# Seven products for a second expert, chosen ahead; the overflow counts among the experts' work

## The chip, the cores and the metric

The kernel runs on one core of a Trainium2 chip. The metric is the time of one execution in microseconds, as the device reports it. Five engines work in parallel, each through its own instructions in program order: TensorE (PE, with its weight loads as PEld), VectorE (DVE), ScalarE (ACT), GpSimd (POOL) and SyncE (SP). They wait for each other and for DMA transfers by semaphores.

## The reference

Sliding-window attention over 8 batches of 8 heads, 576 positions of 64 values, is followed by a mixture of 8 experts in which every token goes to one expert only.

```python
scores = scale * np.matmul(q, k.transpose(0, 1, 3, 2))      # 8 x 8 x 576 x 576
mask = (rel >= 0) & (rel < window)                           # window 128
scores = np.where(mask, scores + bias[None], -1000000000.0)
...
return np.matmul(attn, v).astype(np.float32)
...
expert_idx = np.argmax(logits, axis=1)                       # 4608 tokens of 512, 8 experts
gate_w = probs[np.arange(N), expert_idx]
for e in range(E):
    mask = expert_idx == e
    h = np.maximum(x[mask] @ w1[e], 0.0)                     # w1: 512 x 1024
    out[mask] = gate_w[mask, None] * (h @ w2[e])             # w2: 1024 x 512
```

Nothing fixes beforehand which expert gets how many tokens.

## The kernel before

**Attention.** 36 tiles of 128 tokens pass one after the other through scores, softmax, weights times values, and routing. The rows of a tile go, as two fp16 halves (`hi` and `lo`, whose sum is the fp32 value), into a table `xs` in DRAM that is sorted by expert; GpSimd scatters them (`put`, L940). After 24 tiles the most frequent expert so far is chosen (`head_ops`, eight small VectorE operations, L404 to L411). Its weights are fetched in 16 pieces (`stg`, L985) and split into `hi` and `lo` by ScalarE (L988) and VectorE (L992). Its first 384 rows are computed while attention still runs, to fill TensorE (`head_hidden`, L1020; `head_output`, L1044; `y_head`, L1050). When all tiles are routed, `rank_ops` sorts the experts by their counts.

**Experts.** Each expert has a fixed number of row slots (`SLOTS`, 672 for expert 0, 688 for expert 1) and its turn (`TURNS = [0, 1, 4, 3, 5, 6, 2, 7]`; 0 is the one begun in attention, 1 the next largest by count). SyncE writes a guard of zeros behind the expert's rows (L1350), reads the rows back transposed (`xT`, L1364 and L1367), reads token numbers and gates (`info`), and fetches weights (`ws`, by expert numbers that it loads from memory). Then comes the hidden layer and then the output layer (`ps2` at L1733, 24 matmuls of 512 columns for each block of 128 rows), then `y` and a scattering `put` (L452).

**Two forms of the hidden layer.** `hidden` (L1556) is plain: for each of 8 blocks of 128 hidden units, 12 matmuls over each column block (4 pieces of the sum, each as `hi`·`hi`, `hi`·`lo`, `lo`·`hi`). `seven` (L1576) cuts rows and weights into halves and makes seven products where eight stand in the plain form: for each of 4 pairs of blocks (`ft`), 7 products of 6 matmuls, each over half of the expert's rows. That needs sums of weight quarters (`t1` to `t4`), sums of row halves (`z`, split into `S`), and for every `ft` five combinations of the products on VectorE (`combine`: `u2`, `u3`, `c22`, `c21`, `c12`, L1587 and L1588). `PLAIN = 2` gives the first two experts in turn the plain form. Within an `ft` the products come in the order a(x), b(S2), d(S3), c(S1), a(x), d(x), c(S4); the sixth adds into the bank d, which `u3` must have read before.

**What sets the order.** A planner (`Plan`) takes jobs with an engine, a cost in nanoseconds, what they follow, and a due time, and writes out one static order for every engine; `fill=True` jobs go where the planner sees the engine free. One plan orders attention, a second one the experts.

**The end.** Behind the plan of the experts stand 22 VectorE operations that count the blocks of 128 rows by which an expert overflows its slots (`ovr` to `ooi`, L2041 to L2085), and a loop over these blocks, which these inputs never enter. The last expert also has its output layer in seven products (L1658, with combinations at L1666 and L1667). After the first `put` of the last expert GpSimd drains its queue (`drain`, L1753).

## Time and profile before

| | |
|---|---|
| median of 3 runs | 616.57 us (614.1 to 617.86) |
| profiled execution | 614.46 us |
| its span, first to last instruction | 612.8 us |
| TensorE busy | 581.9 us, 95% |
| VectorE busy | 507.4 us, 83% |
| ScalarE, GpSimd busy | 391.5 us, 315.2 us |
| mean granted TensorE clock | 0.998 of full speed |

The span is what the profile shows; the execution's own time is 1.66 us more. Attention fills the span up to about 262 us, the first expert's remaining rows run to 295, the second expert's from 295 to 349, and the other six to the end. Busy time is an engine's time in instructions. Instructions on one engine overlap a little, so that the start of one to the start of the next can be less than the length of the first.

### The profile page before, as it was taken

The numbers are of one execution on the slowest core, as the hardware profiler recorded it, in microseconds if no ns is written. First come the engines' busy times: TensorE is split into PE (matmuls) and PEld (weight loads), VectorE is DVE, ScalarE is ACT, GpSimd is POOL, SyncE is SP. The second block draws the span as 40 slices with busy tenths as digits, with TensorE's granted clock in tenths as the row PEclk, the third lists the DMA queues.
The fourth block names the chain that finished last, engine by engine and source line by source line (L and its number), as shares of the span: only waits on it lengthen the run. The fifth ranks groups of instructions, "written<-read, shape, count | busy, mean of one in ns | idle before, by whom it ended". The sixth has DMA issues, their size and how long they took to land.

```text
span 612.8 us, 17588 instructions
## 1 busy us (share of the span) xinstructions
PE 581.9 (95%) x6661; PEld 403.3 (66%) x6661; DVE 507.4 (83%) x1259; ACT 391.5 (64%) x895; POOL 315.2 (51%) x486
## 2 busy tenths in 40 slices
PE   7999989999898888999999999999999999999995
PEld 4787777777776666545664584574674854754885
DVE  4988898899999899826489589789899898789692
ACT  6999898899897895415256149149266383376541
POOL 7878779978887888730212402401606214108442
PEclk9999999999999999999999999999999999999999
DMA  9999989999999997779977908908929669424101
GB/s 187 203 174 189 209 184 232 194 203 214 213 187 236 263 173 92 269 196 240 245 211 209 322 15 249 290 1 231 293 55 334 150 150 314 95 76 115 66 2 70
DMA packets 224760, 112.65 MB, mean 184 GB/s; under 512 B 196758, under 2 KB 200342, under 8 KB 224673
## 3 DMA queue, kind: packets, MB, share of 16 engines
q1 hardware_dynamic: 214512, 85.24, 64.5%
q0 software_dynamic: 10160, 26.26, 15.3%
q8 instruction: 53, 0.87, 0.6%
q14 instruction: 35, 0.28, 0.2%
HBM read 72.93 MB, written 19.70 MB: 151 GB/s over the span
## 4 chain that ended last, share of the span: by engine, by line
PE 52%; DVE 24%; ACT 7%; DMA 6%; POOL 5%; issue 4%; POOLq 0%; ACTq 0%; DVEq 0%
PE ps L1733 20%; PE ps7d L1576 5%; PE ps7c L1576 5%; PE ps7a L1576 5%; PE ps L1556 5%; DVE pq L552 4%; DVE nm L693 3%; DVE sc L686 3%; DMA xT<-gx 3%; PE ps7b L1576 3%; ACT pe L700 2%; ACT pq L549 2%; PE ps_t L1723 2%; DMA stg<-moe_w_dram 2%; DVE xf L798 2%
## 5 line engine op out<-in xcount | busy, mean ns | idle before, releaser
L452 POOL DMA_INDIRECT out_dram<-y,ids x32 | 62.1, 1941 | 204.2 <-ACT y L1745 137.0
L700 ACT ACTIVATE pe<-sc,nm 128x128 f32<-128x128 f32 x288 | 84.8, 386 | 6.8 <-DVE nm L693 4.0
L1733 PE MATMUL ps<-w2h,hl 128*128 128x512 f16 x224 | 84.9, 379 | 0.5 <-DVE hl L1697 0.5
L1733 PE MATMUL ps<-w2h,hh 128*128 128x512 f16 x224 | 84.9, 379 | 0.0
L1733 PE MATMUL ps<-w2l,hh 128*128 128x512 f16 x224 | 84.9, 379 | 0.0
L1733 PEld LDWEIGHTS <-hh 128*128 128x128 f16 x448 | 43.7, 98 | 51.7 <-issue 0.8
L1576 PEld LDWEIGHTS <-w1h 128*128 128x128 f16 x672 | 65.7, 98 | 14.8 <-issue 0.3
L552 DVE SCALAR_TENSOR_TENSOR pq<-ptp,pq 128x512 f16<-128x512 f32 x72 | 53.0, 736 | 13.1 <-ACT pq L549 13.0
L549 ACT ACTIVATE pq<-ptp 128x512 f16<-128x512 f32 x72 | 55.4, 769 | 10.9 <-PE ptp L708 7.8
L708 PE MATMUL ptp<-ident,pe 128*128 128x128 f32 x288 | 47.9, 284 | 12.8 <-DVE pq L552 5.1
L676 PE MATMUL sc<-kh,qh 64*64 64x192 f32 (+3 forms) x1280 | 58.1, 289 | 0.0
L693 DVE TENSOR_REDUCE nm<-sc 128x2 f32<-128x256 f32 x144 | 55.8, 411 | 0.6 <-PE sc L676 0.6
L676 PEld LDWEIGHTS sc<-kh,qh 64*64 64x64 f32 (+1 forms) x1280 | 45.0, 139 | 8.8 <-issue 3.6
L825 POOL TENSOR_TENSOR gx<-xf,gx 128x512 f16<-128x512 f32 x36 | 42.3, 1175 | 8.4 <-DVE gx L814 7.4
L708 PEld LDWEIGHTS ptp<-ident,pe 128*128 128x128 f32 x288 | 31.6, 140 | 21.4 <-ACT pe L700 12.4
L1745 ACT ACTIVATE y<-ps,gs 128x512 f32<-128x512 f32 x24 | 16.3, 681 | 45.1 <-PE ps L1733 39.3
L776 PE MATMUL av<-vh,mp 128*128 128x65 f16 (+1 forms) x512 | 42.9, 196 | 1.2 <-POOL mp L728 0.8
L625 POOL TENSOR_TENSOR vo<-ldv,vh 128x512 f16<-128x512 f32 x36 | 40.8, 1137 | 6.3 <-ACT vh L617 5.8
L940 POOL DMA_INDIRECT xs<-gx,di x36 | 36.8, 1021 | 10.6 <-issue 6.0
L1556 PE MATMUL ps<-xT,w1h 128*128 128x288 f16 (+2 forms) x192 | 39.8, 302 | 1.4 <-DMA xT<-xs 1.4
L686 DVE COPY_PREDICATED sc<-mask_full,sc 128x256 f32<-128x256 int32 x96 | 38.2, 418 | 3.1 <-PE sc L676 3.1
L1733 PEld LDWEIGHTS <-hl 128*128 128x128 f16 x224 | 21.9, 98 | 27.7 <-DVE hl L1697 1.5
(315 smaller groups left out, 1743.0 us busy)
## 6 DMA issues: line engine op xcount, KB each, us to landing
ws<-moe_w_dram SPq DMA_DIRECT2D x46, 512.0 KB
ldk<-k_dram SPq DMA_DIRECT2D x32, 256.0 KB
ldq<-q_dram SPq DMA_DIRECT2D x32, 256.0 KB
ldv<-v_dram SPq DMA_DIRECT2D x32, 256.0 KB
...
```

Of the source, the lines that this page charges most:

```text
L452: ins = nc.gpsimd.indirect_dma_start(out[:, :], bass.IndirectOffsetOnAxis(ap=ids, axis=0), y, None, bounds_check=NTOK - 1, oob_is_err=False)
L549: nc.scalar.activation(hi, ps, AF.Copy, scale=scale)
L552: nc.vector.scalar_tensor_tensor(lo, ps, scale, hi, op0=ALU.mult, op1=ALU.subtract)
L676: nc.tensor.matmul(sc[T, hf, j][o, l, c], qT[T]["h"][rows, hp, o], x["h"][rows, hp, c.start + at : c.stop + at], start=False, stop=True, s ...
L686: nc.vector.copy_predicated(ps[:, :, 0:P], m, ps[:, :, P : 2 * P])
L693: nc.vector.tensor_reduce(nm_t[T, hf, j], sc[T, hf, j][:, :, 0:P], axis=AX.X, op=ALU.min)
L700: nc.scalar.activation(pr_t[T, hf][:, 2 * l + j, :], ps[:, l, 0:P], AF.Exp, bias=nm[:, l : l + 1], scale=-1.0)
L708: nc.tensor.transpose(pt[:, i, :], pe[:, i, :], ident)
L776: nc.tensor.matmul(o_, a_, b_, start=False, stop=(n == last), skip_group_check=True)
L1556: nc.tensor.matmul(ps[:, :w], a[:, kt, fs], xx[:, b + kt, c0 : c0 + w], start=(n == 0), stop=(n == len(jobs) - 1))
L1576: nc.tensor.matmul(ps, a[:, idx, c, fs], b[:, c, :], start=(n in OPENS and m == 0), stop=(m == len(jobs) - 1), skip_group_check=True)
L1733: nc.tensor.matmul(ps, x[:, ft, a * P : (a + 1) * P], w[:, ft, c], start=(n == 0), stop=(n == len(jobs) - 1))
```

## The change

Expert 1, the second in turn, gets seven products (`PLAIN = 1`). Nine small VectorE operations (`second_ops`) choose it in attention from the same counts after 24 tiles, and `rank_ops` then keeps it in second place. Its four weight quarters 11, 12, 21 and 22 are fetched at the head of SyncE's stream for the experts, and all four sums of quarters are formed on VectorE (for the other experts `t1` and `t3` are summed by accumulating DMAs). The rows of an expert with seven products are read in two jobs, odd half first, and each half is summed (`rebuild`) as it comes. The overflow counts become filler jobs of the experts' plan, allowed from the second expert's first rows of `hl` on. `y_head` and its `put` go from attention's plan to the experts' plan. The pools stand in another order, so that the weights of the first expert with seven products lie where tiles of attention lay. Attention and experts stand in one region of manual order.

```diff
-PLAIN = 2
+PLAIN = 1
...
+    def second_ops():
+        V = nc.vector
+
+        def k1(nm, dt=F32):
+            return kt_(nm, [P, 1], dt)
+
+        def ke(nm):
+            return kt_(nm, [P, E])
+
+        return [
+            lambda: V.scalar_tensor_tensor(ke("sc"), ke("ho"), -float(PAD), ke("hc"), op0=ALU.mult, op1=ALU.add),
+            lambda: V.tensor_reduce(k1("sm"), ke("sc"), axis=AX.X, op=ALU.max),
+            lambda: V.scalar_tensor_tensor(ke("sd"), ke("sc"), k1("sm"), desc_e, op0=ALU.is_ge, op1=ALU.mult),
+            lambda: V.tensor_reduce(k1("sw"), ke("sd"), axis=AX.X, op=ALU.max),
+            lambda: V.tensor_scalar(ke("so"), ke("sd"), k1("sw"), None, op0=ALU.is_equal),
+            lambda: V.tensor_tensor(ke("si"), ke("so"), iota_e, op=ALU.mult),
+            lambda: V.tensor_reduce(k1("sf"), ke("si"), axis=AX.X, op=ALU.add),
+            lambda: V.tensor_copy(k1("se", I32), k1("sf")),
+            lambda: V.scalar_tensor_tensor(ke("hs"), ke("ho"), 2.0, ke("so"), op0=ALU.mult, op1=ALU.add),
+        ]
...
-            ("DVE", 90, lambda: V.scalar_tensor_tensor(ke("key"), ke("ho"), float(PAD), ke("key"), op0=ALU.mult, op1=ALU.add)),
+            ("DVE", 90, lambda: V.scalar_tensor_tensor(ke("key"), ke("hs"), float(PAD), ke("key"), op0=ALU.mult, op1=ALU.add)),
...
+                prev = [f"head{len(ops) - 2}"]
+                for i, f in enumerate(second_ops()):
+                    J(f"second{i}", "DVE", 90, f, after=prev, due=due("route", u) + 30000 + 150 * i, fill=True)
+                    prev = [f"second{i}"]
             if tail:
-                prev = [done]
+                prev = [done, f"second{len(second_ops()) - 1}"]
...
-            J(f"y{a}", "ACT", 600, lambda a=a: head_y(a), after=[f"out{a}_5", "head_info"] + [f"fetch{i}" for i in range(NP)], makes=[("stg", ("y", a))], uses=[("ps2", a)], due=2e7)
-            J(f"yput{a}", "POOL", 1200, lambda a=a: head_put(a), after=[f"y{a}", (f"put{NT - 1}", ORDER)], uses=[("y", a)], due=3e7)
...
+        steps = [
+            (90, lambda: V.tensor_tensor(ovr, nk, capt, op=ALU.subtract)),
+            (100, lambda: V.tensor_scalar(it128, it, float(P), None, op0=ALU.mult)),
+            (
+                450,
+                lambda: V.tensor_tensor(
+                    big, ovr.unsqueeze(2).to_broadcast([P, E, MAXOV]), it128.unsqueeze(1).to_broadcast([P, E, MAXOV]), op=ALU.is_gt
+                ),
+            ),
+            (450, lambda: V.tensor_reduce(nb, big, axis=AX.X, op=ALU.add)),
...
+            *pick(oe, eb),
+            *pick(oo, base),
+            *pick(on, nk),
...
-        xt, yp, st, ht, wT, wS, zp = (
+        xt, yp, st, wS, zp, wT, ht = (
             pool(*a)
-            for a in (("xt", 2), ("yp", 3), ("wstage", WSTG), ("ht", 1), ("wthird", 1), ("wseven", 1), ("xsum", 1))
+            for a in (("xt", 2), ("yp", 3), ("wstage", WSTG), ("wseven", 1), ("xsum", 1), ("wthird", 1), ("ht", 1))
...
+                number = sel_["se"][0:1, 0:1] if s == TURNS[1] else ebi[0:1, s : s + 1]
+                state[s] = dict(e=nc.sync.value_load(number, min_val=0, max_val=E - 1))
...
-                dl = [nc.sync.dma_start(xx[:, :, t, :], halves[t].bitcast(F16), transpose=True) for t in range(2)]
+                if odd:
+                    xx = xx[:, :, 0 : 2 * n2].rearrange("p k (t j) -> p k t j", t=2)
+                    d = nc.sync.dma_start(xx[:, :, 1, :], halves[1].bitcast(F16), transpose=True)
+                    for p_ in scatters:
+                        sync_dep(d, p_)
+                    state[s]["xT"] = xx
+                    return
+                xx = state[s]["xT"]
+                dl = [nc.sync.dma_start(xx[:, :, 0, :], halves[0].bitcast(F16), transpose=True)]
...
+            if s == TURNS[1]:
+                a, b = {"t1": ("12", "11"), "t3": ("12", "22"), "t2": ("t3", "11"), "t4": ("t2", "21")}[what]
+                nc.vector.tensor_tensor(stage(s, what)[0], ws[s, a], ws[s, b], op=ALU.add)
...
-        def rebuild(s, d):
+        def rebuild(s, t):
             h, xx = SLOTS[s] // 2, state[s]["xT"]
             if s not in zs:
                 zs[s] = zp.tile([P, 2, 2, 2, MH], F32, tag="z", name=f"z_{s}")
-            x, y = (xx[:, b + 2 * d : b + 2 * d + 2, :, 0:h] for b in (0, KT))
-            (nc.gpsimd if XSUM == "POOL" else nc.vector).tensor_tensor(zs[s][:, d, :, :, 0:h], x, y, op=ALU.add)
+            x, y = (xx[:, b : b + KT, t, 0:h] for b in (0, KT))
+            z = zs[s].rearrange("p d k t j -> p (d k) t j")[:, :, t, 0:h]
+            (nc.gpsimd if XSUM == "POOL" else nc.vector).tensor_tensor(z, x, y, op=ALU.add)
...
+            J(f"yh{a}", "ACT", 600, lambda a=a: head_y(a), early=handed["out"][a], makes=[("y", ("yh", a))], uses=[("pre", 8 - HEAD // P + a)], due=-1e6)
+            J(f"yhput{a}", "POOL", 1200, lambda a=a: head_put(a), after=[f"yh{a}"], uses=[("yh", a)], due=-1e6, dma=750)
...
-                first_gets = [("q", what) for what in ("t3", "t1", "11", "21", "22")] if seven_ else [(1, c) for c in range(4)]
+                first_gets = [("q", what) for what in (("t3", "t1", "11", "21", "22") if p > 1 else ("11", "12", "21", "22"))] if seven_ else [(1, c) for c in range(4)]
                 later_gets = [("q", "o" + what) for _, what in first_gets] if s == DEEP else [(2, c) for c in range(4)]
                 for n, (w_, c) in enumerate(first_gets + later_gets):
-                    d = (lead - 3000 * (not seven_) if n < len(first_gets) else m) + 1500 * n
+                    d = (lead if p > 1 else -1e6) + 1500 * n if n < len(first_gets) else (m if p > 1 else 0) + 1500 * n
...
+        caps, steps = over_ops()
+        J("over", "POOL", 600, caps, due=1e6)
+        for i, (ns, f) in enumerate(steps):
+            J(
+                f"over{i}", "DVE", ns, f, after=[f"over{i - 1}" if i else "over", f"qlo{TURNS[PLAIN]}_0a"], port=True, fill=True,
+                due=1e6 + i,
+            )
         plan.run(handed["free"])
...
-    ovr = ot.tile([P, E], F32, name="ovr")
-    nc.vector.tensor_tensor(ovr, nk, capt, op=ALU.subtract)
...
+    with tc.manual_schedule():
+        with ExitStack() as actx:
+            attention(actx)
+        ebi, nki, eb, nk = (sel_[n] for n in ("ebi", "nki", "eb", "nk"))
+        with ExitStack() as mctx:
+            moe(mctx)
```

On SyncE, at the seam between attention and experts, before; `stg` is the last weight piece of expert 0, `xT` the transposed rows of expert 0:

```order
L985 ISA
L985 DMA stg_6898<-moe_w_dram 128x512
L1349 TENSOR_LOAD nki
L1349 ISA x2
L1350 ISA
L1350 DMA xs<-zrow 32x514
L1367 ISA
L1367 DMA_TRANSPOSE xT_7190<-xs 128x8x288
L1383 ISA
L1383 DMA info_7191<-xs 128x2x2
```

and with the change, at the same place:

```order
L1006 ISA
L1006 DMA stg_6916<-moe_w_dram 128x512
L1425 TENSOR_LOAD se
L1425 ISA x2
L1540 ISA
L1540 DMA ws_1_7186<-moe_w_dram 128x2x512
L1540 ISA
L1540 DMA ws_1_7188<-moe_w_dram 128x2x512
L1540 ISA
L1540 DMA ws_1_7190<-moe_w_dram 128x2x512
L1540 ISA
L1540 DMA ws_1_7192<-moe_w_dram 128x2x512
```

The load of the second expert's number and the four quarters now stand ahead of the load of the counts (`nki`), of the guard and of expert 0's transposed rows, which follow behind these rows.

On VectorE, at the end of expert 0's hidden layer, before; `hl` is the low half of its hidden values, `w2l` the low half of expert 1's second weights:

```order
L1697 SCALAR_TENSOR_TENSOR hl_7242<-ps_0_384_7_7380,hh_7241 128x288
L1707 COPY th_7414<-hh_7241 128x256
L1707 COPY tl_7415<-hl_7242 128x256
L1531 SCALAR_TENSOR_TENSOR w2l_7409<-ws_1_0_7276,w2h_7408 128x1024
L1531 SCALAR_TENSOR_TENSOR w2l_7409<-ws_1_1_7282,w2h_7408 128x1024
L1531 SCALAR_TENSOR_TENSOR w2l_7409<-ws_1_2_7406,w2h_7408 128x1024
L1747 TENSOR_SCALAR y_3_7498<-ps_0_3_0_7418,gs_7211 128x512
```

and with the change, from the sum of expert 1's second row half on:

```order
L1590 TENSOR_TENSOR z_7395<-xT_7304 128x4x344
L1626 SCALAR_TENSOR_TENSOR w2l_7492<-ws_1_0_7413,w2h_7491 128x1024
L1596 TENSOR_TENSOR z_7395<-z_7395 128x2x344
L1626 SCALAR_TENSOR_TENSOR w2l_7492<-ws_1_1_7417,w2h_7491 128x1024
L1842 TENSOR_SCALAR y_3_7517<-ps_0_3_0_7466,gs_7263 128x512
L1596 TENSOR_TENSOR z_7395<-z_7395 128x2x344
L1604 TENSOR_TENSOR S_7435<-z_7395,S_7435 128x688
L1596 TENSOR_TENSOR z_7395<-z_7395 128x2x344
L1604 TENSOR_TENSOR S_7435<-z_7395,S_7435 128x688
L1626 SCALAR_TENSOR_TENSOR w2l_7492<-ws_1_2_7433,w2h_7491 128x1024
L1604 TENSOR_TENSOR S_7435<-z_7395,S_7435 128x688
L1626 SCALAR_TENSOR_TENSOR w2l_7492<-ws_1_3_7438,w2h_7491 128x1024
```

Ahead of the same `w2l` splits there is now the summing and splitting of expert 1's rows, in turn with them. Then come eight small operations on `info`, of which the last two are shown with the first combinations of expert 1:

```order
L1510 SCALAR_TENSOR_TENSOR ids_0_7264<-got_5_7605,far_5_7604 64x1
L1511 TENSOR_SCALAR gs_0_7265<-info_7361 64x1
L1682 TENSOR_TENSOR u_1_0_7630<-ps7b_0_7577,s_1_0_7587 128x344
L1682 TENSOR_TENSOR u_1_0_7632<-ps7d_0_7589,u_1_0_7630 128x344
L1683 SCALAR_TENSOR_TENSOR ps7b_0_7577<-ps7c_0_7612,u_1_0_7632 128x344
```

`u` in the third and fourth row are `u2` and `u3`; they stand behind all four `w2l` and all eight `info` operations.

On VectorE, near the end of the last expert, before; `u` and `r` are the combinations `u2` and `u3` of the output layer, the rows of L2072 and L2073 are overflow counts:

```order
L2073 TENSOR_REDUCE oe<-in_11244 128x44
L1666 TENSOR_TENSOR u_7_('o', 0)_11063<-ps2b_0_11041,r_10728 128x256
L2072 TENSOR_TENSOR in_11244<-inn,base 128x352
L2083 CAST oei<-oe 128x44
L2073 TENSOR_REDUCE oo<-in_11244 128x44
L1666 TENSOR_TENSOR r_10728<-ps2d_0_11054,u_7_('o', 0)_11063 128x256
L2072 TENSOR_TENSOR in_11244<-inn,nk 128x352
L1667 SCALAR_TENSOR_TENSOR ps2b_0_11041<-ps2c_0_11027,r_10728 128x256
L1666 TENSOR_TENSOR ps2e_0_10990<-ps2e_0_10990,r_10728 128x256
```

and with the change:

```order
L1727 SCALAR_TENSOR_TENSOR hs_3_11069<-ps7c_3_11014,hs_3_11069 128x256
L1761 TENSOR_TENSOR u_7_('o', 0)_11151<-ps2b_0_11129,r_10816 128x256
L1761 TENSOR_TENSOR r_10816<-ps2d_0_11142,u_7_('o', 0)_11151 128x256
L1762 SCALAR_TENSOR_TENSOR ps2b_0_11129<-ps2c_0_11115,r_10816 128x256
L1761 TENSOR_TENSOR ps2e_0_11078<-ps2e_0_11078,r_10816 128x256
L1762 SCALAR_TENSOR_TENSOR ps2c_0_11115<-ps2c_0_11115,u_7_('o', 0)_11151 128x256
```

The counts are gone from between the combinations.

## Rows read from the trace of the kernel before

**Rows 1.** The page, busy time of each engine, its share of the span, and instructions.
```profile
PE 581.9 (95%) x6661; PEld 403.3 (66%) x6661; DVE 507.4 (83%) x1259; ACT 391.5 (64%) x895; POOL 315.2 (51%) x486
```

**Rows 2.** Busy time by stretch: length; PE, PEld, DVE, ACT, POOL; clock, DMA share, GB/s.
```profile
200.00:240.00 40.00, 33.69 (x662) 26.08 (x662) 37.50 (x117) 34.32 (x94) 33.62 (x54) 1.00 0.96 183
...
260.00:270.00 10.00, 10.00 (x48) 4.47 (x46) 2.06 (x13) 1.37 (x2) 4.39 (x8) 1.00 0.55 151
...
400.00:460.00 60.00, 60.00 (x413) 40.23 (x411) 55.34 (x108) 34.85 (x62) 13.11 (x8) 1.00 0.55 150
```

**Rows 3.** The chain of work, 288 to 352 us: start, length, what.
```profile
294.93 28.00 PE ps L1556 x192
322.93 25.90 PE ps L1733 x120
348.83 0.69 PE ps7a L1576 x6
```

**Rows 4.** What TensorE waited for, 225 to 613 us: total, times, longest.
```profile
PE ps L1556 <- DMA xT<-xs: 1.4, 1, 1.4
...
PE ps2c L1658 <- DVE ps2b L1667: 0.9, 1, 0.9
...
PE ps L1733 <- DVE hl L1697: 0.5, 1, 0.5
```

**Rows 5.** The chain of work, 235 to 300 us.
```profile
249.46 5.61 DMA stg<-moe_w_dram
...
271.41 7.28 DMA out_dram<-y_head,ids_head
278.87 1.06 ACT w1h L1533
...
285.27 1.47 PE ps L1733 x6
286.77 8.16 PE ps L1733 x37
```

**Rows 6.** SyncE's queue in order of time, 248 to 300 us: start, time to issue, what.
```profile
263.41 0.38 SPq L1350 DMA_DIRECT2D xs<-zrow  x1
265.90 2.36 SPq L1367 DMA_TRANSPOSE xT<-xs  x1
...
273.24 0.36 SPq L1350 DMA_DIRECT2D xs<-zrow  x1
...
279.72 6.95 SPq L1367 DMA_TRANSPOSE xT<-xs  x1
```

**Rows 7.** VectorE by shape, 255 to 345 us: count, busy us, mean ns, idle before.
```profile
L1531 DVE SCALAR_TENSOR_TENSOR w2l<-ws,w2h 128x1024 f16<-128x1024 f32 x8 | 9.6, 1219 | 5.9 <-ACT w2h L1533 5.9
...
L1697 DVE SCALAR_TENSOR_TENSOR hl<-ps,hh 128x336 f16<-128x336 f32 x8 | 3.8, 502 | 1.3 <-ACT hh L1699 1.2
...
L1501 DVE TENSOR_TENSOR z<-z 128x544 f32<-128x544 f32 x4 | 2.9, 718 | 0.0
...
L1495 DVE TENSOR_TENSOR z<-xT 128x1152 f32<-128x1152 f16 x2 | 2.6, 1352 | 0.0
```

**Rows 8.** VectorE in order of time, 586 to 613 us.
```profile
596.40 0.52 DVE L2072 TENSOR_TENSOR in<-inn,nk 128x352 f32<-128x352 f32 x1
596.84 0.43 DVE L1667 SCALAR_TENSOR_TENSOR ps2b<-ps2c,r 128x256 f32<-128x256 f32 x1
```

**Rows 9.** GpSimd in order of time, 597 to 613 us.
```profile
598.78 1.00 POOL L452 DMA_INDIRECT out_dram<-y,ids  x1 [7.16 <-ACT y L1689]
...
608.37 0.97 POOL L452 DMA_INDIRECT out_dram<-y,ids  x1 [0.30 <-issue]
```

**Rows 10.** VectorE by shape, 190 to 215 us: the choice of the first expert.
```profile
L406 DVE SCALAR_TENSOR_TENSOR hd<-hc,hm,desc_e 128x8 f32<-128x8 f32 x1 | 0.5, 465 | 0.0
...
L411 DVE CAST he<-hf 128x1 int32<-128x1 f32 x1 | 0.1, 142 | 0.0
```

**Rows 11.** Line 992 on VectorE, 190 to 260 us: shortest, median and longest in ns.
```profile
L992 DVE SCALAR_TENSOR_TENSOR w1l<-stg,w1h x8: 655/717/2420, 205.3 to 242.6; 128x512 f16<-128x512 f32 x8
```

180 lines of the change are left out of this document (97 added, 83 removed).

## Prediction

> **What bounds the kernel now.** The first view is the busy time of the page: TensorE works 581.9 of 612.8 us [rows 1]. So time can leave the kernel in two ways only: fewer matmuls, or fewer of the 31 us in which TensorE stands still. The second view is the same by stretches [rows 2]. TensorE is short of work in attention (33.69 of 40 us at 200 to 240, where VectorE is busy 37.50) and near the end; from 300 to 580 it never waits for more than fractions of a microsecond. VectorE stands nearly idle around the seam (2.06 of 10 us at 260 to 270) and is nearly full later (55.34 of 60 us at 400 to 460). The third view, the chain of work, shows the second expert as two unbroken pieces of matmuls, 28.00 us hidden and 25.90 us output, with the next expert right behind [rows 3]. The fourth, TensorE's waits, has two of about a microsecond that the change touches: 1.4 for the first expert's transposed rows and 0.9 for a combination in the last expert's output [rows 4].
>
> **Fewer matmuls.** The plain hidden layer of expert 1 is 192 matmuls in 28.00 us, 0.1458 us each [rows 3], over 352 or 336 columns, 344 in the mean. Seven products make 4 x 7 x 6 = 168 matmuls of 344 columns: 24.5 us. The 24 that are gone are worth **-3.5 us**, since all of them lay on the path.
>
> **The counts at the end.** `c22` starts at 596.84 behind a count that started at 596.40 [rows 8]; that one costs 0.44 us of VectorE, and three such stand between `u2` and `c22`. TensorE's wait of 0.9 is for this `c22` [rows 4]. Without the counts that wait goes, and the first `put` of the last expert (598.78), whose `y` hangs on the same chain, moves by the three counts, 1.3 us. The last `put` at 608.37 follows it by a drain and three equal steps [rows 9], not by TensorE. I take **-1.2**, between 0.9 and 1.3. What is late next is `y` of the last product, about 1 us earlier too. Moved into the middle, the counts are 22 operations, about 8 us of VectorE; their price stands in the term on experts 1 to 4.
>
> **The end of expert 0.** Before, the third `y_head` waits on ScalarE's stream for a `put`: a weight split starts only at 278.87, when the transfer begun at 271.41 has landed, and the evictions of expert 0 stand behind it [rows 5]. Its output then stops for `hl`: 0.5 us in the waits [rows 4], and the 43 matmuls from 285.27 take 9.66 us up to 294.93, where at 25.90 / 120 = 0.2158 us each they would take 9.28, 0.4 more. With the change `y_head` has its own buffers and the seven weight splits need no `put`. I take **-0.9**, at worst 0: by the list below the fifth `hl` is done near 284.6, and the output wants it about 1 us later. A late odd half of expert 1's rows, whose sum stands between these `hl`, would cost 1:1 beyond that cover.
>
> **The choice of the second expert** adds nine small VectorE operations where VectorE is full [rows 2]. The like operations of the first choice take 0.14 to 0.47 us [rows 10]. Nine are 1.3 to 4.2 by these ends; most are of the cheap kind, and two neighbours overlap by 0.09. I take **+1.1**, ends 0 (if they fall into VectorE's gaps) and 1.8. Queued behind them are the tiles' `pq` and `xf`, for which TensorE waits. Line 992, with two operands in SBUF, takes 655 ns at best and 2420 at worst in this stretch, where GpSimd is busy 33.62 of 40 us [rows 2, 11]. [...]
>
> **The fetch of four quarters ahead** is queued on SyncE behind the last `stg` piece (issued near 249.46), where SyncE has nothing until the guard at 263.41 [rows 5, 6]. Four transfers of 512 KB run there beside the last scatters of `xs`. The transposed reading of expert 0's rows cannot start before the guard and the last scatter have landed, 265.90. What such a block can cost is seen later: a guard behind four weight fetches, at 273.24, lets the transposed reading start only at 279.72, 6.5 us instead of 2.5 [rows 6]: 4.0 us more. Here the fetches have 14 us of cover, so I take **+0.5**, ends 0 and 4.0. In return expert 1's rows no longer stand behind those fetches.
>
> **The start of expert 1** is the largest new risk. All weight splits of expert 1 must wait until the scatters have left the tiles that they lie on, about 265.9 [rows 6]. From the first `w1l` to `u3` VectorE then has, at mean duration less 0.09 of overlap [rows 7]: 7 `w1l`, 4 `w2l` and 2 sums at 1.13 = 14.7; 8 `hl` of expert 0 at 0.40 (the wider one less a little) = 3.2; two row sums of 1376 elements, 1.35 at 1152, about 1.5 = 3.0; four `z` and four `S` of 688, 0.72 at 544, about 0.78 = 6.2; the small operations on `info`, the tail copies and one `y` about 3.4; `u2` and `u3` 0.8. Sum 31.3 us. It starts at 265.9 + 1.06 for ScalarE's first split [rows 5], 266.95. ScalarE must make five more splits (0.96 each) and two `y_head` before VectorE's second `w1l`, which leaves VectorE idle some 2.7 us. So `u3` comes at 266.95 + 31.3 + 2.7 = 300.95. TensorE begins expert 1 at 294.93 - 0.9, runs five products of 6 x 0.1458 = 0.875 us, and wants `u3` at 298.4. Loss **+2.5 us**. If each duration were 0.05 shorter, or if the idle time were filled, nothing would be lost; with full durations (some 50 operations times 0.09) it is 7. The `info` and `w2l` operations ahead of `u2` are what makes it late. Within the later `ft` VectorE needs 5 combinations and 4 `hl`, 9 times about 0.45, 4.1 us, in 6.1 us of matmuls: no more loss there.
>
> **From expert 1 to expert 4.** VectorE's list in expert 1's output is 13 operations at 1.13 (two sums, seven `w1l`, four `w2l`), two row sums of expert 3 at 1.3, eleven of about 0.65 (`z`, `S`), two copies, seven counts (about 1.5 us) and eight `info` operations (1.2): 27 us. It begins some 2.5 us into the output's 25.90, when the last `hl` is done, and ends where expert 4's sixth product wants `u3`, 5 x 0.69 us after the output [rows 3], less 0.8: 26.0 us of room. That is 1.0 late; I take **+0.9**, ends 0 and 4.4 (no overlap at all). The other counts fall where VectorE is up to 92% busy [rows 2], two or three to an expert; I count 0 for them, and 1 as the bad end.
>
> **Sum.** -3.5 - 1.2 - 0.9 + 1.1 + 0.5 + 2.5 + 0.9 = **-0.6 us**. The profiled execution's 614.46 (its span of 612.8 and 1.66 around it) becomes 613.9. It stands 2.1 below the median of the runs, so I move the median: 616.57 - 0.6 = **616.0**. The seven products pay, but VectorE hands most of it back.
>
> **Rivals.** (a) *VectorE is in time.* The overlap is larger or the idle time is filled, and both VectorE terms vanish: -0.6 - 3.4 = -4.0, 612.6. For it: VectorE's idle room at 260 to 280 is real. Against it: the splits may not start before the scatters end. With the choice of the second expert free as well, -5.1, 611.5. (b) *VectorE becomes the bound.* From the start of expert 1 to expert 4 it has about 31 + 16 + 27 us of work and gets some 84 us, less than 1.2 times; if its operations keep their full duration instead of overlapping (about 130 operations x 0.09 = 11 us), the start loses 7 (4.5 more than forecast) and the next seam 4.4 (3.5 more): -0.6 + 8.0 = +7.4, 624.0, slower. This decides from the point where the spacing is more than 0.04 above what rows show. Against it: in the rows the same kinds of operations follow each other with the overlap. (c) *The fetches are in the way.* Expert 0's rows start 4.0 late: -0.6 + 3.5 = +2.9, 619.5. For it, the guard of 273.24; against it, 14 us of cover. [...] (d) *The change does nothing for TensorE* is excluded: the matmuls that are gone are gone whatever the tokens are, since the slots are fixed.
>
> **How the numbers follow.** Forecast, near -0.6: 0.52. (a) 0.24, (c) 0.12, (b) 0.12. A measurement of this kernel can tell about 1%, 6.2 us. Faster than 610.4 needs (a) with every other cost at its low end, 0.10. Slower than 622.7 is (b) and the worst of (c), 0.14. Within 1%: 0.76. The range leaves out those ends: 610.5 to 621.5.
>
> **What would show it.** The hidden layer of expert 1 should be 168 matmuls, 24.5 us plus a wait for `u3` of about 2.5 in its first sixth product; no wait for the `c22` of the last output; expert 0's output without the gap near 285; the wait for expert 0's rows still near 1.4; the last `put` 1.2 us nearer to the start of the last output. The prediction is wrong if TensorE waits in experts 4 and 3 as well, or if attention grows by over 2 us.

## The result, and the profile after

The changed kernel takes 618.86 us (median of 14 runs, 616.3 to 621.78) against 615.55 us for the kernel before on the same chip: 1.0053 times as long, interval 1.0035 to 1.0071. Forecast was 0.6 us less; it is 3.3 us more. The profiled execution took 617.29 us, its span is 615.6, where that of before is 612.8.

The page's busy time answers to [rows 1]:

```profile
PE 581.0 (94%) x6637; PEld 401.7 (65%) x6637; DVE 532.4 (86%) x1302; ACT 402.2 (65%) x909; POOL 336.1 (55%) x483
```

TensorE has its 24 matmuls less, VectorE 25 us more. Where the time went is read by stages, each from the start of its first matmul to that of the next one, in the timelines of both kernels:

| stage | before | after | difference | forecast |
|---|---|---|---|---|
| attention and seam, up to expert 0's remaining rows | 271.77 | 273.99 | +2.22 | +1.6 |
| expert 0's output | 11.23 | 11.24 | +0.01 | -0.9 |
| expert 1's hidden layer | 28.00 | 27.97 | -0.03 | -1.0 |
| expert 4's seven products | 19.46 | 20.76 | +1.30 | +0.9 |
| seven products of experts 6 and 7 | 37.59 | 38.36 | +0.77 | 0 |
| last output, and what follows TensorE's end | 25.80 | 24.26 | -1.54 | -1.2 |

The stages left out (expert 0's hidden layer, 11.77; all other outputs; experts 3, 5 and 2) are equal to 0.02 us. TensorE's waits, 284 to 400 us (total, times, longest), answer to [rows 4]:

```profile
PE ps7d L1671 <- DVE u L1682: 2.1, 2, 1.7
PE ps7b L1671 <- DVE S L1604: 1.2, 1, 1.2
PE ps L1828 <- DVE hl L1792: 0.7, 1, 0.7
PE ps7a L1671 <- ACT s L1685: 0.6, 1, 0.6
```

The wait for the last `c22` is gone, as forecast. In its place stand waits for VectorE at expert 1 (`S` 1.2, `u` 1.7) and at expert 4 (`s` 0.6, `u` 0.4), and the wait for `hl` in expert 0's output is still there. VectorE in order of time, 264 to 305 us (in brackets its idle time, and what ended it):

```profile
270.18 1.23 DVE L1573 SCALAR_TENSOR_TENSOR w1l<-ws,w1h 128x1024 f16<-128x1024 f32 x1 [1.87 <-ACT w1h L1575]
271.32 1.22 DVE L1547 TENSOR_TENSOR ws_t<-ws_t,ws 128x1024 f32<-128x1024 f32 x1
275.11 1.22 DVE L1573 SCALAR_TENSOR_TENSOR w1l<-ws_t,w1h 128x1024 f16<-128x1024 f32 x1 [2.57 <-ACT w1h L1575]
...
285.71 1.58 DVE L1590 TENSOR_TENSOR z<-xT 128x1376 f32<-128x1376 f16 x1
287.21 0.81 DVE L1792 SCALAR_TENSOR_TENSOR hl<-ps,hh 128x288 f16<-128x288 f32 x2
...
304.29 0.52 DVE L1682 TENSOR_TENSOR u<-ps7d,u 128x344 f32<-128x344 f32 x1
```

Its weight splits begin 3.2 us later than forecast (266.95). It stands idle for ScalarE 1.87 us before the first split and 2.57 us behind it, a row sum of 1.58 us stands ahead of the `hl` for which expert 0's output waits, and `u3` is done at 304.81, 3.9 us later than forecast. ScalarE there:

```profile
269.09 2.95 ACT L1575 ACTIVATE w1h<-ws 128x1024 f16<-128x1024 f32 x3 [8.42 <-DMA xs<-gx,di]
```

It starts when the last scatter of `xs` has landed (the idle time in brackets). Its first three splits are of 11, 21 and 22, while VectorE's list goes on with `t3`. The chain of work shows what bounds the next seam; TensorE's 25.90 us of output are not on it:

```profile
341.86 0.95 DVE w2l L1626
342.99 3.49 DVE w2l L1626 x3
346.49 1.27 DVE z L1590
...
351.00 0.67 DVE z L1596
355.65 0.85 PE ps7d L1671 x6
```

Something not foreseen stands beside it. GpSimd, 320 to 352 us, and ScalarE, 348 to 356 us:

```profile
332.94 15.79 POOL L473 DMA_INDIRECT out_dram<-y,ids  x1 [22.87 <-ACT y L1840]
349.03 1.67 POOL L473 DMA_INDIRECT out_dram<-y,ids  x1 [0.31 <-DMA ws<-moe_w_dram]
```

```profile
352.75 1.29 ACT L1840 ACTIVATE y<-ps,gs 128x512 f32<-128x512 f32 x2 [8.75 <-DMA out_dram<-y,ids]
353.94 0.39 ACT L1685 ACTIVATE s<-ps7a 128x272 f32<-128x272 f32 x1
```

A `put` that elsewhere takes 1.0 us [rows 9] takes 15.79. The kernel before has three such puts too, of 6.97, 7.37 and 11.53 us, at places where TensorE waits for nothing; the longest of them:

```profile
554.95 11.53 POOL L452 DMA_INDIRECT out_dram<-y,ids  x1 [1.94 <-ACT y L1745]
```

In expert 1's output it matters. The three `y` buffers stay taken, ScalarE waits 8.75 us for one, and expert 4's first `s` stands behind that. VectorE at the moment when the `put` ends (348.73):

```profile
346.40 1.35 DVE L1590 TENSOR_TENSOR z<-xT 128x1152 f32<-128x1152 f16 x1
347.67 0.16 DVE L1362 TENSOR_TENSOR tab_first<-nk,tab_first 128x8 f32<-128x8 f32 x1
347.75 1.35 DVE L1590 TENSOR_TENSOR z<-xT 128x1152 f32<-128x1152 f16 x1
```

VectorE has run long operations without a gap since 327.2. The first short one, a count, starts at 347.67; the `put` ends 1.06 later, about its ordinary duration.

At the seam, the last scatter, and SyncE's guard and transposes [rows 6]:

```profile
264.55 0.96 POOL L961 DMA_INDIRECT xs<-gx,di  x1 [0.19 <-issue]
```

```profile
265.48 0.38 SPq L1432 DMA_DIRECT2D xs<-zrow  x1
269.10 2.82 SPq L1458 DMA_TRANSPOSE xT<-xs  x1
```

### The profile page after: what moved, and what is told of

Same layout as the page of the kernel before. It is cut to its first block, busy times and chain, and to the rows that moved or that the text cites. A ratio compares the mean times of both kernels' runs of the same rounds, so it can differ in the third digit from the quotient of the medians.

```text
span 615.6 us, 17590 instructions
## 1 busy us (share of the span) xinstructions
PE 581.0 (94%) x6637; PEld 401.7 (65%) x6637; DVE 532.4 (86%) x1302; ACT 402.2 (65%) x909; POOL 336.1 (55%) x483
## 3 DMA queue, kind: packets, MB, share of 16 engines
HBM read 72.93 MB, written 19.70 MB: 150 GB/s over the span
## 4 chain that ended last, share of the span: by engine, by line
PE 45%; DVE 31%; DMA 8%; ACT 7%; POOL 4%; issue 4%; SPq 0%; POOLq 0%; ACTq 0%; DVEq 0%
PE ps L1828 14%; PE ps7c L1671 6%; PE ps7d L1671 6%; PE ps7a L1671 5%; DVE pq L573 4%; DMA xT<-gx 3%; DVE nm L714 3%; DVE w1l L1573 3%; PE ps7b L1671 3%; DVE sc L707 2%; DMA stg<-moe_w_dram 2%; DVE w2l L1626 2%; DVE z L1596 2%; PE sc L697 2%; PE ps_t L1818 2%
## 5 line engine op out<-in xcount | busy, mean ns | idle before, releaser
L473 POOL DMA_INDIRECT out_dram<-y,ids x32 | 84.2, 2632 | 185.6 <-ACT y L1840 150.8
L1671 PEld LDWEIGHTS <-w1h 128*128 128x128 f16 x784 | 76.7, 98 | 24.4 <-issue 4.6
L1840 ACT ACTIVATE y<-ps,gs 128x512 f32<-128x512 f32 x27 | 18.3, 681 | 48.1 <-PE ps L1828 32.3
L1708 ACT ACTIVATE hh<-ps7b 128x264 f16<-128x264 f32 (+5 forms) x28 | 13.5, 482 | 50.3 <-DVE ps7b L1683 50.3
L1671 PEld LDWEIGHTS <-w1l 128*128 128x128 f16 x392 | 38.3, 98 | 10.7 <-issue 1.5
L1671 PE MATMUL ps7a<-xT,w1h 128*128 128x264 f16 (+5 forms) x224 | 43.2, 285 | 0.6 <-ACT s L1685 0.6
L1671 PE MATMUL ps7c<-S,w1h 128*128 128x264 f16 (+5 forms) x224 | 43.2, 285 | 0.1
```

The costliest lines, as they stand in the source:

```text
L473: ins = nc.gpsimd.indirect_dma_start(out[:, :], bass.IndirectOffsetOnAxis(ap=ids, axis=0), y, None, bounds_check=NTOK - 1, oob_is_err=False)
L1671: nc.tensor.matmul(ps, a[:, idx, c, fs], b[:, c, :], start=(n in OPENS and m == 0), stop=(m == len(jobs) - 1), skip_group_check=True)
```

## The experiments

Every comparison ran beside the kernel before on one chip. "Work" is the time from the start of expert 0's hidden layer to TensorE's end (334.87 us in the kernel before, 335.83 in the changed one), which leaves attention out; the stages are those of the table above.

| run | time, before | ratio and interval | expert 1 hidden | expert 4 | expert 3 | work |
|---|---|---|---|---|---|---|
| after_again | 622.69, 622.17 | 1.0004 (0.999 to 1.0019) | 27.97 | 20.83 | 20.58 | 335.56 |
| w2_late | 624.94, 622.17 | 1.0043 (1.0026 to 1.006) | 24.50 | 25.32 | 21.47 | 337.66 |
| counts_tail | 623.6, 622.17 | 1.002 (1.0005 to 1.0035) | 27.97 | 21.18 | 20.58 | 336.00 |
| b_counts | 624.09, 622.17 | 1.0032 (1.0014 to 1.005) | 28.00 | 19.46 | 25.00 | 337.76 |
| after_c2 | 625.15, 624.0 | 1.003 (1.0006 to 1.0053) | 27.98 | 20.76 | 20.58 | 335.63 |
| t3_first | 623.42, 624.0 | 1.0 (0.9979 to 1.0021) | 24.61 | 20.76 | 20.58 | 333.02 |
| no_counts | 624.05, 624.0 | 1.0001 (0.9979 to 1.0023) | 27.97 | 21.18 | 20.58 | 335.48 |
| fetch_late | 636.2, 624.0 | 1.0196 (1.0162 to 1.0229) | 36.52 | 25.20 | 21.48 | 349.86 |
| gaps | 618.18, 615.5 | 1.003 (1.0005 to 1.0056) | 27.98 | 21.05 | 23.07 | 338.11 |
| t3_yh_gaps | 615.16, 615.5 | 0.9993 (0.9966 to 1.002) | 26.89 | 21.04 | 20.58 | 333.73 |
| best | 618.34, 615.5 | 1.005 (1.0027 to 1.0072) | 25.54 | 20.37 | 27.74 | 338.39 |
| b_choice3 | 620.73, 615.5 | 1.0093 (1.0061 to 1.0124) | 28.00 | 19.46 | 20.58 | 337.91 |
| nc_breath1 | 614.81, 615.0 | 1.0 (0.9983 to 1.0017) | 27.97 | 19.94 | 20.58 | 333.65 |
| nc_breath2 | 616.04, 615.0 | 1.0025 (1.0004 to 1.0046) | 27.96 | 20.14 | 20.58 | 334.73 |
| t3_yalt | 614.58, 615.0 | 1.0006 (0.9985 to 1.0027) | 26.61 | 19.71 | 22.02 | 334.31 |
| t3_yalt_tail | 612.29, 615.0 | 0.9958 (0.9938 to 0.9979) | 26.23 | 19.70 | 20.58 | 331.48 |
| all4 | 624.08, 622.52 | 1.003 (1.0009 to 1.0052) | 27.04 | 22.78 | 20.58 | 335.54 |
| t3_tail_breath | 619.88, 622.52 | 0.9969 (0.995 to 0.9987) | 26.53 | 19.95 | 20.58 | 336.51 |

**The changed kernel again**, unaltered (after_again, after_c2).

> The changed kernel unaltered, as the base for the runs beside it. Ratio to the kernel before 1.005 (1.003 to 1.008). In its first profile the attention was 1.2 us later than before from about 80 us on, in a stretch where both programs are the same; theory A (that is chance of the transfers) expects this part to differ again, between 0 and 1.5 us; theory B (the change itself slows early attention, for instance by other addresses) expects 1.2 again.

> The changed kernel as it is, on the chip of the next three runs, so that they can be set against it. If the loss of half a per cent lies in the experts (about 1 us by the stages) and in a seam that costs 1 us more, it stands 1 to 3 us above the kernel before here too. If the 2.2 us that the first comparison showed in attention were the chance of the transfers, it stands within 1 us of it, as in the run on the chip before this one.

Its work is 0.7 to 1.0 us above that of the kernel before in all three, so the experts' share of the loss is firm. Its parts vary a little: expert 0's output took 11.60 and 11.72 us here, and the seven products of experts 6 and 7 37.67 and 37.68, so that the 0.77 of the table is mostly chance. What is left of the medians' difference, for attention, the seam and the puts behind TensorE's end, differs from one comparison to the next: 2.3 us of the first one's 3.3, -0.2 in the second and 0.4 in the third.

**Moving VectorE's work behind `u3`** (w2_late). The four `w2l` splits and `info` of expert 1, and the first row sum of expert 4, follow expert 1's first `c22`.

```diff
-  after=[f"whi{w_}_{s}_{c}"], ...
+  after=[f"whi{w_}_{s}_{c}"] + (before(f"c22{s}_0") if p == 1 else []), ...
```

> The four w2l splits and the info operations of expert 1, and the first sum of expert 4's rows, stand on VectorE behind expert 1's first c22. Theory A (the VectorE list ahead of u3 is what eats the saved matmuls): the waits for S (1.2) and u3 (1.7) vanish, expert 1's hidden layer takes 24.5 to 25.5 us instead of 27.98, and the kernel is 2 to 3 us faster than the changed one, ratio to before 0.999 to 1.002. Rival B (VectorE is full from expert 1 to expert 4, so what is put off comes back): hidden 25, but output of expert 1 or hidden of expert 4 longer by 1.5 to 3 us, ratio 1.004 or more.

The hidden layer takes 24.50 us, all that the matmuls save, and expert 4 gives it back and more. TensorE's wait there, and the `put`:

```profile
PE ps7a L1671 <- ACT s L1685: 3.9, 1, 3.9
```

```profile
336.26 18.69 POOL L473 DMA_INDIRECT out_dram<-y,ids  x1 [20.25 <-ACT y L1840]
```

The wait is not for VectorE but for ScalarE's `s`, which stands behind a `y` that waits 11.03 us for its buffer, and the `put` is held up longer than in the changed kernel. Expert 4 lost more than that wait, 5.9 us; the last section tells why.

**The counts** (counts_tail, b_counts, no_counts): the counts of the changed kernel back at the end; the kernel before with the counts as fillers and nothing else; the changed kernel without counts (number of blocks set to zero).

```diff
+  after=[...] + before(f"hs{DEEP}_3_4"), due=0.0,     # counts_tail
```

> The changed kernel with the 22 overflow counts back between the last combinations of the last expert. Theory A (as fillers they cost about 1 us in experts 4 to 7, at the end they cost 1.5): 0.5 us slower than the changed kernel, ratio to before 1.006. Rival B (as fillers they are what slows experts 4, 6 and 7, 2.0 us in the profile): 0.5 to 1 us faster than the changed kernel, ratio 1.003 to 1.005, and expert 4's hidden layer back at 19.5.

> The kernel before with that one part of the change: the counts as fillers from the third expert on, nothing else. Theory A: the last output loses its wait of 0.9, and VectorE has room, so 1.0 to 1.5 us faster than before, ratio 0.998. Rival B (as fillers they delay combinations): 0 to 1 us slower, ratio 1.000 to 1.002.

> The counts of overflow blocks are left out (the number of blocks is set to zero), 22 operations and about 8 us of VectorE. Theory A (the counts as fillers cost what the later experts lost): expert 4's seven products fall from 20.8 to 19.5 us, the seven of expert 6 and 7 by 0.3 together, and the time is 1.5 to 2 us below the changed kernel's; the hidden layer of expert 1 stays at 28.0, since no count stands before it. Rival B (the counts fall into VectorE's spare time, and expert 4 waits for the weight splits and sums that were late already): expert 4 stays at 20.5 or more, and the time is within 0.5 us of the changed kernel's.

Without any count expert 4 still takes 21.18 us, as in counts_tail: the `put` ahead of it takes 17.71 us, and rival B holds for expert 4. As fillers in the kernel before, the counts cost 4.4 us at expert 3, while the last output and what follows it fall by 1.20 us (19.60 to 18.50, and 6.20 to 6.10). GpSimd and VectorE there:

```profile
386.26 12.02 POOL L452 DMA_INDIRECT out_dram<-y_t,ids  x1 [2.74 <-DVE w1l L1547]
398.26 2.60 POOL L1524 DMA_DIRECT2D ws_t<-moe_w_dram  x2
```

```profile
404.19 1.22 DVE L1527 TENSOR_TENSOR ws_t<-ws_t,ws 128x1024 f32<-128x1024 f32 x1 [2.36 <-DMA ws_t<-moe_w_dram]
```

A held `put` again, with another victim: the fetches that add up `t1` and `t3` stand behind it on GpSimd, come late, and VectorE waits for them ahead of `u3`. Back at the end of the changed kernel (counts_tail) the counts cost 0.28 us of the last output (18.78 against 18.50) and about 0.2 behind it.

**The seam** (fetch_late, b_choice3): the quarters of expert 1 fetched after expert 0's transposes; and the kernel before with the nine operations of the choice three times over, their results unused.

```diff
-  number = sel_["se"][0:1, 0:1] if s == TURNS[1] else ebi[0:1, s : s + 1]
+  number = ebi[0:1, s : s + 1]                         # fetch_late
+  for i, f in enumerate(sum((second_ops(r) for r in range(3)), [])):   # b_choice3
```

> The four quarters of expert 1 are fetched after expert 0's transposed rows, by the number from the final ranking; the nine operations of the choice stay. Theory A (the fetches share the DMA engines with the last scatters and make them land late): the scatters at the seam land in 3 to 4 us instead of 6 to 7, and expert 0's hidden layer starts 1 to 2 us earlier, while expert 1 pays for the later quarters, 5 to 9 us of wait before its sixth product: the time is 3 to 8 us above the changed kernel's. Rival B (the fetches cost the seam nothing and what attention lost is chance): expert 0 starts where it does in the changed kernel on this chip, within 0.5 us, and the time is 5 to 9 us above it.

> The kernel before with the nine operations of the choice of a second expert added three times over (27 operations on VectorE, none of whose results is used) at the place where the change has them. Theory A (each small operation costs its time, since VectorE is full there, as the prediction has it): the last scatter starts 3 us later than in the kernel before, and the time is 3 us above it, 1.005. Rival B (they fall into VectorE's gaps and what attention lost in the first comparison is the chance of its transfers): within 1 us of the kernel before, 1.000 to 1.0015.

From the last scatter's start to the start of the transposes, and from there to TensorE's start, the changed kernel takes 4.55 and 4.89 us, the kernel before 3.68 and 5.87, fetch_late 3.60 and 6.46 (rows 264.55 and 269.10 above and TensorE's start at 273.99; for fetch_late 271.57, 275.17 and 281.63). So with the early fetches the last scatters land 0.9 us later, and the transposes, beside which the fetches ran before, take 1.0 us less: neither theory was right. For TensorE, which waits for the transposes, the sum is no longer with early fetches (9.44, 9.55 and 10.06 us); VectorE's list, whose weight splits wait for the scatters, starts 0.9 us later. fetch_late's loss is that of expert 1 (36.52) and expert 4 (25.20), by quarters that come too late. The 27 operations make the last scatter start 1.6 us later than in the kernel before, and TensorE's start 2.6 us: 0.5 to 0.9 for nine. The medians agree: of their 5.2 us, 2.8 stand behind TensorE's start, which leaves 0.8 for nine. Expert 0's output lost 3.05 us more, because the `put` of the third `y_head`, on which ScalarE waits in the kernel before [rows 5], came later too.

**VectorE's order at the seam** (t3_first): expert 1's splits begin with `t3`.

```diff
-  for n, what in enumerate(("11", "t3", "t1", "t2", "21", "22", "t4")):
+  for n, what in enumerate(("t3", "11", "t1", "t2", "21", "22", "t4") if p == 1 else (...)):
```

> The weight splits of expert 1 begin with t3 and not with 11, and nothing else is edited. Theory A (VectorE starts its list for expert 1 late because it stands idle at the seam for ScalarE's splits, 1.9 and 2.6 us in the changed kernel): with t3 first the sums t2 and t4 can run while ScalarE splits, the 2.6 us of idle time go, u3 comes 2 to 3 us earlier, the hidden layer of expert 1 takes 24.5 to 25.9 us instead of 28.0, and expert 4 stays at 20.8: the kernel is 2 to 3.5 us faster than the changed one. Rival B (VectorE has no room between the start of expert 1 and expert 4, as when the w2 splits were moved): the hidden layer gets shorter, but expert 4's seven products get longer by the same 2 to 3 us, and the time stays within 0.7 us of the changed kernel's.

Theory A holds for the stages: the hidden layer takes 24.61 us, expert 4 no more than in the changed kernel, expert 0's output falls to 10.36, by the 0.9 us forecast for it, and the median is 1.7 us below the changed kernel's. But expert 0's hidden layer grew by 1.67 us to 13.44. TensorE had stood still for 2.5 us for the transposed rows, and its granted clock then fell to 0.50 of full speed for some 3 us. Windows (length; PE, PEld, DVE, ACT, POOL; granted clock, DMA share, GB/s):

```profile
281.20:282.70 1.50, 1.50 (x9) 1.08 (x10) 1.19 (x9) 0.65 (x1) 0.09 (x1) 0.70 0.53 194
282.70:284.20 1.50, 1.50 (x8) 0.88 (x6) 1.06 (x1) 0.40 (x2) 0.00 (x0) 0.50 0.11 25
284.20:285.20 1.00, 1.00 (x6) 0.61 (x5) 0.96 (x2) 0.95 (x2) 0.00 (x0) 0.50 0.33 48
285.20:288.00 2.80, 2.80 (x24) 2.26 (x23) 2.17 (x4) 0.82 (x2) 0.00 (x0) 1.00 1.14 239
```

The expectations of the next versions blame the `put`s of `y_head` for this 1.7; what cost it was the clock: 0.30 lost of 1.5 us and 0.50 of 2.5 us make 1.7 by these rows. From the start of the transposes to TensorE's start it took 5.91 us here, and 4.73 with `y_head` behind the splits (t3_yh_gaps, below), which speaks for these `put`s as the cause of the longer wait, by one trace each. Those 1.67 us also gave VectorE time: from expert 0's hidden layer to the end of expert 1's, the changed kernel takes 50.98 us, t3_first 48.41, t3_yh_gaps 49.02. The late list cost 4.4 us there, 3.5 in expert 1 and 0.9 that expert 0's output did not gain; 2.0 to 2.6 of it came back with the new order of the splits.

**The held `put`** (gaps, nc_breath1, nc_breath2). In gaps the first seven counts stand one behind each weight split of expert 4. The other two are no_counts with a tiny operation behind each of these splits, and differ only in it:

```diff
+  nc.vector.tensor_copy(tiny[:, 0:1], tiny[:, 1:2])                           # nc_breath1
+  nc.vector.tensor_tensor(tiny[:, 0:1], tiny[:, 1:2], tiny[:, 2:3], op=ALU.add)  # nc_breath2
```

> The first seven counts of the changed kernel move up by some 15 us: one stands behind each weight split of expert 4 in expert 1's output, instead of all behind the last of them. Nothing is taken away or added. Theory P (a put on GpSimd cannot finish while VectorE runs its long operations back to back, 15.8 us in the changed kernel; the three y buffers then stay taken, ScalarE waits 8.75 us for one, and the s of expert 4 stands behind that): each small count lets a put through, the puts of expert 1 take 1 to 4 us, ScalarE does not wait for a buffer, and expert 4's seven products fall from 20.8 to 19.5 us. Theory V, as in the prediction (expert 4 waits because VectorE's list is late): the list is as long as before, so the seven products stay at 20.5 to 21, or grow by up to 1 us, since seven counts now stand before u3.

> The kernel without the counts, with a tiny VectorE operation (a copy of one column, one operand read from SBUF) behind each of the eleven weight splits of expert 4 in expert 1's output; it adds about 1 us to VectorE and is left out of nothing else. In the kernel without the counts GpSimd's put takes 17.7 us there, ScalarE waits 9.2 us for its y buffer and expert 4's seven products take 21.18 us. Theory P1 (VectorE's operations that read two operands from SBUF, run back to back, hold GpSimd's put up, and an operation with one operand lets it through): the puts take 1 to 4 us each, ScalarE waits for no buffer, and the seven products take 19.5 to 19.8 us. Rival P2 (the put is held up by something else, as the transfers of weights in that stretch): the put still takes 15 us or more and the seven products 21 us.

> The same as the run before it, but the tiny operation is an addition of two columns (two operands read from SBUF). Theory P1: it lets nothing through; the put takes 17 us or more and the seven products of expert 4 21 us or more, as without it. Rival P3 (any short operation, or any change from one operation to the next, lets the put through): as with the copy, puts of 1 to 4 us and 19.5 to 19.8 us.

GpSimd's first `put` in expert 1's output: no_counts, nc_breath1, nc_breath2, gaps.

```profile
339.17 17.71 POOL L473 DMA_INDIRECT out_dram<-y,ids  x1 [25.19 <-ACT y L1840]
```

```profile
332.24 3.63 POOL L473 DMA_INDIRECT out_dram<-y,ids  x1 [23.95 <-DVE tab_first L1576]
```

```profile
332.51 3.66 POOL L473 DMA_INDIRECT out_dram<-y,ids  x1 [25.31 <-DVE tab_first L1576]
```

```profile
332.57 5.89 POOL L473 DMA_INDIRECT out_dram<-y,ids  x1 [23.29 <-DVE tails L1363]
```

VectorE's first tiny operation within that `put`, in nc_breath1 and nc_breath2:

```profile
334.82 0.15 DVE L1576 COPY tab_first<-tab_first 128x1 f32<-128x1 f32 x1
```

```profile
335.12 0.15 DVE L1576 TENSOR_TENSOR tab_first<-tab_first 128x1 f32<-128x1 f32 x1
```

Both `put`s end 1.05 us after that start (335.87 and 336.17). Expert 4 falls from 21.18 to 19.94 and 20.14 us, though VectorE has eleven operations more. So VectorE's unbroken run holds the `put`, and P2 is out. What P1 expected of nc_breath2 did not come. But that any short operation lets the `put` through (P3) is not so either. Two counts that stand within the `put` of 5.89 us in gaps, on VectorE:

```profile
335.22 0.52 DVE L1366 TENSOR_TENSOR tails<-tab_first,tails 128x352 f32<-128x352 f32 x1
337.42 0.51 DVE L1370 TENSOR_REDUCE tab_first<-tails 128x8 f32<-128x352 f32 x1
```

Behind the start of the first, which reads two operands from SBUF, the `put` goes on for 3.25 us. It ends 1.04 us after the start of the second, which reads one. The other traces agree. In the 20 profiles of this document 83 `put`s took over 3 us, and each ended 0.86 to 1.06 us, about its ordinary duration, after the first of three things on VectorE: an operation that reads at most one operand from SBUF, as a cast, a reduction or an eviction from PSUM (43 times); a pause of 0.03 us or more between two operations (30 times); or a two-operand operation of about 0.16 us, on 1 or 8 columns (10 times, nc_breath2 among them). Fifteen two-operand operations of 0.2 to 0.5 us stood within such `put`s and ended none. (One operation that came 0.39 us after a `put`'s start did not end it.) So P1 is right but for the very shortest operations. The row sums, weight splits and additions of the changed kernel's list all read two operands from SBUF.

In gaps ScalarE no longer waits for a buffer, but expert 4 stays at 21.05: with seven counts ahead of it, VectorE's list is as late as the `put` was. Theory V was right on that part. In the changed kernel `s` is done at 354.33 and VectorE's list ahead of `u2` at 354.58, so both causes end together, and taking one away shows the other.

**Both causes together.** All versions have t3 first and `y_head` behind the splits; "yalt" gives expert 1's evictions to ScalarE and VectorE in turn, as before the change, "tail" has the counts at the end, best and all4 move `info` of expert 1 behind `c22`; t3_yh_gaps and best have the first seven counts as in gaps, all4 has "yalt" and "tail" too.

```diff
-  e = ("ACT", "DVE")[(n_out + i) % 2 if p < PLAIN or two else 0]
+  e = ("ACT", "DVE")[(n_out + i) % 2 if p < 2 or two else 0]      # yalt
```

> Three edits on the changed kernel: t3 is split first for expert 1, the three y_head stand behind ScalarE's splits 11, t1 and t2, and the first seven counts stand between the weight splits of expert 4. If the three causes found so far add up (the idle time in VectorE's list at the seam; the puts of y_head beside expert 0's transposed rows, which cost the earlier trial of t3 first 1.7 us; the put that is held up), expert 0's hidden layer takes 11.8 us, its output 10.4, expert 1's hidden layer 24.6, expert 4's seven products 19.5: 331 us from expert 0's hidden layer to TensorE's end against 335.7 in the changed kernel and 334.9 in the kernel before, so 4 us below the kernel before, 0.993 of it. If the time saved comes back at another place (the rival), it stands at 0.998 or more.

> The same three edits, and the eight small operations on expert 1's info stand behind c22 of its first column tile and not ahead of u2. If VectorE's list is still late by a little (0.1 to 1 us) with the three edits alone, this gives it back and the kernel is the fastest, 0.992 to 0.994 of the kernel before. If these small operations are what lets the put at the start of expert 1 through (it ended right behind them in the changed kernel), the put is held longer, a y buffer with it, and ScalarE's s waits at the start of expert 1 or in its first column tiles: 1 us slower than without this edit.

> Three edits on the changed kernel: t3 first, the three y_head behind ScalarE's splits, and the evictions of expert 1's output taken by ScalarE and VectorE in turn, as in the kernel before, where in the changed kernel ScalarE takes them all. An eviction by VectorE reads PSUM and one operand, and the put behind it starts where VectorE has just let go: the puts of expert 1 take 1 to 3 us, as in the kernel before (1.8 and 2.2). By the put theory expert 4's seven products take 19.5 to 20.5 us and the time is 0.994 to 0.997 of the kernel before; by the list theory the three evictions (0.7 us each) make VectorE's list later by 2 us, the seven products take 21 to 23 us, and the time is that of the kernel before or above it.

> The three edits of the run before it, and the counts back between the last combinations, where they cost 0.3 us of the last output in the earlier trial. With neither a put that is held up nor counts ahead of u3, expert 4's seven products should take 19.5 us by both theories, and experts 3, 5, 6, 2 and 7 no more than in the kernel before: 331 us from expert 0's hidden layer to TensorE's end against 334.9 in the kernel before, 0.993 to 0.995 of it, the fastest of all. If VectorE is short of time by itself in experts 1 and 4 (the rival), expert 1's hidden layer or expert 4 still loses 1 to 2 us, and the time is 0.997 to 1.0.

> The fastest version so far (t3 first, the three y_head behind ScalarE's splits, expert 1's evictions in turn, the counts at the end) with the eight small operations on expert 1's info behind c22 of its first column tile. By the list theory VectorE's u3 of expert 1 comes about 1.3 us earlier and its hidden layer takes 24.6 to 25.0 us instead of 26.2; with no counts in the middle nothing takes it back, and the work from expert 0's hidden layer to TensorE's end is 330 us, against 331.5 there: 0.993 to 0.995 of the kernel before. By the put theory these operations were what let the put at the start of expert 1 through; without them it takes over 8 us, the later puts and the fetches behind them move, and expert 4 or 3 gives the 1.3 us back or more.

> t3 first, the three y_head behind ScalarE's splits and the counts at the end, but expert 1's evictions all on ScalarE as in the changed kernel; in their place a one-column copy stands behind each of expert 4's weight splits on VectorE. If short operations let the puts through as well as the evictions do, the puts of expert 1 take 1 to 4 us and expert 4's seven products 19.5 to 20.2 us, with 1 us of VectorE's time in place of 2: 0.994 to 0.996 of the kernel before. If the evictions on VectorE were needed to free ScalarE or PSUM in time, expert 4's products take 20.5 us or more.

t3_yalt_tail is 0.2 to 0.6% faster than the kernel before; t3_tail_breath, with short operations in place of evictions, 0.1 to 0.5%. In best and all4 the `put`s met other stretches of VectorE's list, one was held anew, and the gain was lost. In best the fetches of `t1` and `t3` stand behind such a `put` on GpSimd, and VectorE waits for them. GpSimd and VectorE at expert 3:

```profile
374.12 16.50 POOL L473 DMA_INDIRECT out_dram<-y,ids  x1 [22.88 <-ACT y L1840]
```

```profile
398.10 1.23 DVE L1553 TENSOR_TENSOR ws_t<-ws_t,ws 128x1024 f32<-128x1024 f32 x1 [4.42 <-DMA ws_t<-moe_w_dram]
```

In all4 two `put`s of 10.01 and 9.15 us follow each other in expert 1's output, and ahead of `u` stands an eviction by VectorE that needs the buffer of the second, which ended at 355.96 (VectorE is idle for 2.73 us up to 357.78; the profile names a matmul as the last to be waited for): expert 4 takes 22.78. In the profiled execution of t3_tail_breath, the slowest of its twelve, a `put` of 12.57 us costs expert 7 4.5 us; how often that happens was not tried.

## Why the prediction was wrong

The sum was 0.6 us less than before, and 3.3 more was measured. The mechanism named as the largest risk, VectorE's list at the start of expert 1, was right, and the step that failed is the size of that term. Against the forecast the profile is off by 1.0 us in that term, 0.9 at the end of expert 0, 0.6 in attention and the seam, 0.4 from expert 1 to expert 4 and 0.8 in experts 6 and 7; the counts gave 0.3 more than forecast.

- **Fewer matmuls** (-3.5) was right: 24.50 and 24.61 us in the two runs where VectorE was in time. **The counts at the end** (-1.2) was right: 1.54 in the changed kernel's profile, and 1.20 in b_counts, which moves the counts alone.
- **The start of expert 1** (+2.5) is the step that failed by size: 3.5. The list itself was counted well: from the first `w1l` to `u3` it took 34.6 us where 31.3 + 2.7 = 34.0 stood. Its idle time was 2.57 us at the place forecast and 0.54 more ahead of an `S`. What the step had wrong is where the list starts against TensorE. It took the time of the kernel before for the splits' start, and they start when the scatters have landed, TensorE when the transposed rows have. The first split came 3.2 us later than forecast, but TensorE's first matmul on these rows only 2.2 us later (273.99 against 271.77), because the early fetches put the scatters' landing 0.9 us back and made the transposes faster. So of the 1.9 us by which this term and the next are off together, 1.0 is the list's start and 0.6 its length.
- **The end of expert 0** (-0.9) measured 0. The step named what undid it: the row sum between the `hl`s, 1:1 beyond a cover of 1 us. The late list used that cover up. With the list in time (t3_first) it measured -0.88.
- **From expert 1 to expert 4** (+0.9) measured +1.3, by the mechanism named, VectorE's list, and by a second one that ends at nearly the same time and was not named: the held `put`, its buffer, ScalarE's `s`. The list alone accounts for the size: `s` is done at 354.33, and VectorE comes to `u2` from its own list at 354.62. The held `put`s of the kernel before were there to be read.
- **The choice** (+1.1) and **the fetch** (+0.5): 0.5 to 0.9 by b_choice3, and -0.1 from the last scatter to TensorE's start (what the fetch cost stands in the start of expert 1). That leaves 1.4 to 1.8 of the 2.2 us lost up to there without a shown cause, in a comparison in which attention grew by over 2 us, one of the prediction's own signs of being wrong. In the other two comparisons the changed kernel lost, beside its work, -0.2 and +0.4 us, so it may be the chance of attention's transfers; this stays open.
- **The later experts** (0) measured 0.8 in the first trace of the changed kernel and 0.1 in the two others.
- Of the rivals, (b), VectorE as the bound, came true in kind: the chain of work runs through VectorE at 276 to 301 and 327 to 351 us. It did so by a late start and idle time, not by operations that fail to overlap. (c) named the right place, but from the last scatter's start TensorE's rows took no longer (9.44 us against 9.55); the scatters landed 0.9 us later, and VectorE's list paid. (a) is what t3_yalt_tail comes near to: 2.7 us below the kernel before, where (a) had 4.0.

The prediction had operations of VectorE with two operands in SBUF beside a busy GpSimd in its rows (up to 2420 ns [rows 11]), weighed them in the term on the choice only, and asked nothing about the `put`s. A `put` did not wait for one operation of VectorE: in the changed kernel the longest beside it took 1.35 us, the `put` 15.79. None of the 83 long `put`s ended while two-operand operations of 0.2 us or more followed each other without a pause. `tensor_tensor` alone held one as well: in no_counts VectorE ran nothing else for the last 3.2 us before the pause that let the `put` of 17.71 us through.
